# Linear attention ahead of a routed feed-forward: two of three key groups subtracted on GpSimd behind a ScalarE copy, and the attention's order planned anew

## The chip, the cores and the metric

The kernel runs on one core of one Trainium2 chip. The metric is the device time of one execution in microseconds (us). The engines are TensorE (PE), VectorE (DVE), ScalarE (ACT), GpSimd (POOL) and SyncE (SP, which here only issues transfers).

## The reference

For q, k, v of 8 batches, 8 heads, 576 positions and 64 columns, and a 64x128 matrix `w_phi`:

```python
def phi(x):
    proj = einsum('bhsd,df->bhsf', x, w_phi)
    proj = proj - max(abs(proj), axis=-1, keepdims=True)
    return concatenate([exp(proj), exp(-proj)], axis=-1)   # 256 features
q_p, k_p = phi(q), phi(k)
kv = einsum('bhsf,bhsd->bhfd', k_p, v)
z = sum(k_p, axis=2)
x = (q_p @ kv) / (q_p @ z + 1e-6)
```

Each of the 4608 rows of x (512 columns) is then given to one of 8 experts with a fixed capacity by its gate logits, and passes that expert's two-layer ReLU network. The change touches the attention alone.

## The kernel before

The attention works through 16 units, each two batches by two heads (the loop `for u in range(NU): unit(u)`). A unit's 576 positions are nine tiles of 64, taken in three groups of three (`SG`, line 134). For a unit:

- SP loads K and Q in pieces of 72 KB that already stand half transposed (`raw`, line 108), and V (`loadv`). Each has two buffers.
- DVE finishes the transposes of K and Q (`kT`, `qT`, line 158).
- PE projects a group of K or Q with `w_phi` into a pair of PSUM banks (line 169). All PSUM of this stage is four such pairs, `NG=4`.
- DVE takes the absolute maximum along the features (`kgm`, `qgm`, line 173) and subtracts it (`kgt`, `qgt`, line 176); both read the 128x768 projection from PSUM, and the subtraction gives the pair free.
- For K, ACT takes Exp of plus and minus `kgt` (`kP`, line 188); POOL adds the nine tiles up in eight additions (`ks`, lines 194 and 195); PE multiplies `kP` with V (line 204).
- For Q, PE transposes `qgt` (line 248) and ACT takes both Exps out of PSUM (`qP`, line 252).
- ACT copies the K-V product out of PSUM (`kvT`, line 208), PE turns it into the layout of the last product and appends the gate weights (`bd`, line 220), ACT copies that (`kz`, line 223); PE reduces `ks` over partitions (`z`, line 235), and DVE adds it to `kz` (line 237).
- PE forms numerator, denominator and logits (line 265); DVE divides (lines 269 to 280, `xp`); SP stores x; POOL sums the logits (lines 290, 292).

Units overlap. The order on each engine is made by the class `Plan`: each step has an engine, a duration in ns, a due time in us, steps that it depends on, and buffers that it takes and frees. `Plan.order` simulates the engines with these numbers and always takes the step that can start first, preferring early due times; the steps are then recorded in that order, and each engine runs its own list strictly in sequence. The due times are the constants of `ATT` (line 856): `TI` is the pitch of units, the others say where in a unit a step is due. Between the steps of units 1 to 3 stand 40 small steps (`init`, line 298) that build constants for the routing (lines 351 to 415): POOL makes a ramp, DVE casts or scales it. Behind the last unit of each pair of batches stand twelve DVE steps that prepare the routing (`pr`) and a count on PE.

Of the kernel before, what the change touches and what calls it, by code (L numbers as in the profile page):

```python
# [89 lines left out]
def attention(ctx, tc, nc, q, k, v, w_phi, w_gate, xs, L, C, xp, cfg={}, after=None, later=None, count=None, init=iter(())):  # L90

    B,H,S,D=q.shape
    NB=B//2; NP=H//2; NU=NB*NP
# [44 lines left out]
    def unit(u):  # L138
        bp,hp=divmod(u,NP)
        t0=u*d['TI']  # L140
        def add(name,eng,dur,due,fn,deps=(),mode=None,slot=(),frees=(),lat=None,after=0.):
            P.add((name,u),eng,dur,t0+due,fn,[(x,u) for x in deps],
                  lat={'PE':170.,'DVE':95.,'ACT':100.,'POOL':30.,'SP':0.}[eng] if lat is None else lat,mode=mode,slot=slot,frees=frees,after=after)
        def slots(*l): return tuple((kd,n,(kd,u) if len(z)==0 else (kd,u)+tuple(z)) for kd,n,*z in l)
        first=u==0
        if not first:
            add('ldk','SP',5200.,-d['ldk'],lambda x: loadx('k',k,u),slot=slots(('ki',2)),lat=4500.)
            add('ldq','SP',5200.,-d['ldq'],lambda x: loadx('q',q,u),slot=slots(('qi',2)),lat=4500.)
            add('ldv','SP',1300.,-d['ldv'],lambda x: loadv(u),slot=slots(('vi',2)),lat=4500.)
        else:  # L150
            for nm in 'kqv': add('ld'+nm,'SP',0.,-d['ldk'],lambda x: None,slot=slots((nm+'i',2)))

        def blocks(nm,aft):

            for bi in range(2):
                def f(x,bi=bi):
                    if bi==0: T[nm+'T',u]=sb.tile([128,2,9,32,2],F32,name=nm+'T',bufs=2)
                    V.transpose(T[nm+'T',u][:,bi].rearrange('p s t l -> p l s t'),T[nm,u][:,bi])
                add((nm+'t',bi),'DVE',640.,d[nm+'t']+.7*bi,f,['ld'+nm],slot=slots((nm+'T',2)) if bi==0 else (),frees=((nm+'i',u),),after=aft[bi] if first else 0.)
        def project(nm,g,s0,s1,due,src):  # L160
# [13 lines left out]
            def sub(x):  # L174
                t=T[nm+'t',u,g]=sb.tile([128,2,n,128],F32,name=nm+'t',bufs=3)
                V.tensor_sub(t,vw(),T[nm+'m',u,g].to_broadcast([128,2,n,128]))  # L176
# [4 lines left out]
        blocks('k',(7500.,8500.))  # L181
        for g,(s0,s1) in enumerate(SG):
# [6 lines left out]
            add(('ke',g),'ACT',2*ac(256*n,False),due+2.6,ex,[('kgs',g)],slot=slots(('kP',2)) if g==0 else (),frees=(('kgt',u,g),))  # L189
            def ad(x,s0=s0,s1=s1,g=g):  # L190
                if g==0: T['ks',u]=sb.tile([128,2,256],F32,name='ks',bufs=2)
                ks=T['ks',u]; kP=T['kP',u]
                for s in range(s0,s1):
                    if s==1: G.tensor_add(ks,kP[:,0],kP[:,1])  # L194
                    elif s>1: G.tensor_add(ks,ks,kP[:,s])  # L195
            add(('ad',g),'POOL',1300.*(n-(g==0)),due+4.,ad,[('ke',g)]+([('ad',g-1)] if g else []),frees=(('kP',u),),slot=slots(('ks',2)) if g==0 else ())
# [45 lines left out]
        for g,(s0,s1) in enumerate(SG):
# [10 lines left out]
            add(('T',g),'PE',2*n*109.+20.,due+d['T'],tr,[('qgs',g)],'A',slots(('g',NG,'T',g)),(('qgt',u,g),))  # L253
            add(('ex',g),'ACT',2*ac(256*n),due+d['T']+.8,ex,[('T',g)],slot=slots(('qP',d['nqP'],g)),frees=(('g',u,'T',g),))
        lastu=u==NU-1
        for g,(j0,j1) in enumerate(JG):
# [656 lines left out]
```

## Time and profile before

| what | us |
|---|---|
| median of 3 runs (809.74 to 812.13) | 810.55 |
| the profiled execution | 809.45 |
| its span, first to last instruction | 807.7 |
| PE busy in the span | 756.6 (94%) |
| DVE busy | 573.1 (71%) |
| ACT busy | 327.3 (41%) |
| POOL busy | 263.8 (33%) |
| first numerator of the attention (unit 0) starts | 33.60 |
| last numerator (unit 15) starts | 303.64 |

The first 310 us of the span are the attention, the rest routing and feed-forward. Shares over the whole span mix these stages: DVE is 94% busy in the attention's middle. A busy PE is not PE at its peak, since matmuls are pipelined and their ends are modelled; the distance from one burst to the next tells more. A line like `L176` is line 176 of the kernel before.

### The profile page before, as it was taken

The numbers are of one execution on the slowest core, as the hardware profiler recorded it, in microseconds if no ns is written. First come the engines' busy times: TensorE is split into PE (matmuls) and PEld (weight loads), VectorE is DVE, ScalarE is ACT, GpSimd is POOL, SyncE is SP. The second block draws the span as 40 slices with busy tenths as digits, with TensorE's granted clock in tenths as the row PEclk, the third lists the DMA queues.
The fourth block names the chain that finished last, engine by engine and source line by source line (L and its number), as shares of the span: only waits on it lengthen the run. The fifth ranks groups of instructions, "written<-read, shape, count | busy, mean of one in ns | idle before, by whom it ended". The sixth has DMA issues, their size and how long they took to land.

```text
span 807.7 us, 25190 instructions
## 1 busy us (share of the span) xinstructions
PE 756.6 (94%) x10718; PEld 653.4 (81%) x10718; DVE 573.1 (71%) x1407; ACT 327.3 (41%) x579; POOL 263.8 (33%) x295
## 2 busy tenths in 40 slices
PE   5888999999999996799999999999999999999995
PEld 3777887888888785488798798798898898897983
DVE  5798899999999885787686686586586685550400
ACT  2544555665554463143343243234334333441410
POOL 2664676655666560200401302203103104302011
PEclk9999999999999997699999999999999999999998
DMA  8868668668777311433424314405314424701300
GB/s 130 146 119 161 119 121 155 128 118 165 126 152 143 77 33 32 134 135 116 128 83 144 127 58 161 161 16 180 138 54 137 138 89 131 271 1 45 119 27 32
DMA packets 225344, 91.89 MB, mean 114 GB/s; under 512 B 191905, under 2 KB 208321, under 8 KB 225233
## 3 DMA queue, kind: packets, MB, share of 16 engines
q1 hardware_dynamic: 214400, 70.74, 37.5%
q0 software_dynamic: 6096, 18.97, 7.0%
q8 instruction: 84, 1.38, 0.7%
q10 hardware_dynamic: 4736, 0.59, 0.5%
q14 instruction: 28, 0.22, 0.1%
HBM read 71.39 MB, written 18.87 MB: 112 GB/s over the span
## 4 chain that ended last, share of the span: by engine, by line
PE 58%; issue 14%; DVE 10%; POOL 5%; SPq 5%; DMA 4%; ACT 3%; POOLq 0%; DVEq 0%; ACTq 0%
PE h L788 19%; PE y L817 17%; PE g L265 5%; SPq L114 4%; PE g L204 3%; PE g L169 3%; POOL ks L195 3%; PE y L832 2%; PE g L248 2%; ACT qP L252 2%; DMA qi<-in_q_dram 2%; PE h L763 2%; POOL out_dram L846 1%; PE rps L541 1%; DMA ki<-in_k_dram 1%
## 5 line engine op out<-in xcount | busy, mean ns | idle before, releaser
L195 POOL TENSOR_TENSOR ks<-ks,kP 128x512 f32<-128x512 f32 x112 | 142.8, 1275 | 9.9 <-ACT kP L188 1.3
L788 PE MATMUL h<-xh,w1h 128*128 128x272 f32 (+3 forms) x512 | 144.5, 303 | 0.2 <-DVE xl L766 0.2
L788 PE MATMUL h<-xh,w1l 128*128 128x272 f32 (+3 forms) x512 | 143.0, 299 | 0.0
L846 POOL DMA_INDIRECT out_dram<-ysb,idx x40 | 40.4, 1010 | 206.2 <-ACT ysb L840 166.7
L799 ACT ACTIVATE fh<-h 128x272 fp32r<-128x272 f32 (+2 forms) x128 | 49.2, 384 | 134.8 <-PE h L788 123.6
L817 PE MATMUL y<-w2h,fl 128*128 128x512 f32 x256 | 102.2, 399 | 0.0
L817 PE MATMUL y<-w2l,fh 128*128 128x512 f32 x256 | 101.9, 398 | 0.0
L817 PE MATMUL y<-w2h,fh 128*128 128x512 f32 x256 | 101.5, 397 | 0.0
L788 PEld LDWEIGHTS h<-xh,w1h 128*128 128x128 f32 x512 | 96.5, 189 | 2.1 <-issue 1.2
L758 POOL DMA_INDIRECT xg<-xs,idx x40 | 39.5, 987 | 177.2 <-issue 141.3
L788 PEld LDWEIGHTS h<-xh,w1l 128*128 128x128 f32 x512 | 96.7, 189 | 0.0
L803 DVE SCALAR_TENSOR_TENSOR fl<-h,fh 128x272 fp32r<-128x272 f32 (+2 forms) x128 | 52.8, 420 | 55.8 <-ACT fh L799 42.4
L788 PE MATMUL h<-xl,w1h 128*128 128x272 f32 (+3 forms) x512 | 91.8, 298 | 0.0
L188 ACT ACTIVATE kP<-kgt 128x768 f32<-128x768 f32 x96 | 74.5, 835 | 32.9 <-DVE kgt L176 32.5
L265 PE MATMUL g<-kz,qP 128*64 128x73 f32 x2304 | 77.6, 227 | 3.9 <-issue 2.1
L265 PEld LDWEIGHTS g<-kz,qP 128*64 128x64 f32 x2304 | 74.9, 136 | 7.6 <-issue 4.2
L252 ACT ACTIVATE qP<-g 128x768 f32<-128x768 f32 x96 | 71.9, 820 | 11.2 <-PE g L248 11.1
L788 PEld LDWEIGHTS h<-xl,w1h 128*128 128x128 f32 x512 | 75.6, 189 | 0.0
L204 PE MATMUL g<-kP,vi 64*64 64x256 f32 x1152 | 69.7, 382 | 2.4 <-DVE xp L280 1.3
L840 ACT COPY ysb<-y 128x512 f32<-128x512 f32 (+1 forms) x40 | 21.8, 544 | 101.1 <-PE y L817 70.9
L204 PEld LDWEIGHTS g<-kP,vi 64*64 64x64 f32 x1152 | 48.1, 135 | 13.8 <-issue 2.1
L194 POOL TENSOR_TENSOR ks<-kP 128x512 f32<-128x512 f32 x16 | 20.5, 1280 | 109.2 <-ACT kP L188 109.2
(179 smaller groups left out, 1329.2 us busy)
## 6 DMA issues: line engine op xcount, KB each, us to landing
raww<-in_moe_w_dram SPq DMA_DIRECT2D x64, 512.0 KB, 6.2
vi<-in_v_dram SPq DMA_DIRECT2D x32, 288.0 KB, 4.6
xs<-xp SPq DMA_DIRECT2D x32, 288.0 KB, 3.8
ki<-in_k_dram SPq DMA_DIRECT2D x124, 72.0 KB, 3.2
qi<-in_q_dram SPq DMA_DIRECT2D x124, 72.0 KB, 3.3
xg<-xs,idx POOLq DMA_INDIRECT x40, 3.6
out_dram<-ysb,idx POOLq DMA_INDIRECT x40, 3.5
ki<-in_k_dram ACTq DMA_DIRECT2D x4, 72.0 KB, 5.3
```

The source lines that it names most:

```text
L114: eng.dma_start(t[64*a+32*db:64*a+32*db+32,bi],o)
L188: for i in range(2): A.activation(o[:,:,:,128*i:128*i+128],t,AF.Exp,scale=1.0-2*i)
L195: elif s>1: G.tensor_add(ks,ks,kP[:,s])
L204: PE.matmul(p[64*a:64*a+64,i,0:256],v_[r,a,s,:],kP[r,s,a,:],start=s==0,stop=s==8,skip_group_check=True)
L252: for fh in range(2): A.activation(t[:,fh].rearrange('p a s t -> p a (s t)'),p,AF.Exp,scale=1.0-2*fh)
L265: PE.matmul(p[64*ab:64*ab+64,a,73*(j-j0):73*(j-j0)+73],T['qP',u,j//3][:,fh,a,j%3,64*ab:64*ab+64],T['kz',u][:,ab,fh,a,:],start=fh==0,stop=f ...
L758: G.indirect_dma_start(out=T['xg',r][0:n,bb,:],out_offset=None,in_=xs,in_offset=bass.IndirectOffsetOnAxis(ap=T['idx',r][0:n,bb,:],axis=0))
L788: PE.matmul(p,ws[:,k,o:o+128],xx[:,k,o1:o2],start=n==0,stop=n==11)
L799: A.activation(hh[:,f,o1:o1+m1],p[:,0:m1],AF.Relu)
L803: V.scalar_tensor_tensor(hl[:,f,o1:o1+m1],p[:,0:m1],0.0,hh[:,f,o1:o1+m1],op0=OP.max,op1=OP.subtract)
L817: PE.matmul(p,hx[:,f,o:o+128],ws[:,f%2,:],start=n==0,stop=n==23)
L846: st=G.indirect_dma_start(out=ov,out_offset=bass.IndirectOffsetOnAxis(ap=iv,axis=0),in_=yv,in_offset=None)
```

## The change

For the first two K groups of every unit but the first, the subtraction is split. ACT copies the projection from PSUM into `kgt` behind the maximum, which gives the PSUM pair free, and POOL subtracts the maximum from `kgt` in place (new lines 185 and 188). The third K group and the Q groups keep the DVE subtraction. In the plan, the additions on POOL become eight steps of their own with a due time `ad`; several durations are set anew; the steps `boot` and `aboot` count the first loads, by keeping SP and ACT occupied to 10.1 and 10.3 us; and all due times in `ATT` are new. New line numbers are 14 to 15 higher than old ones around the K groups.

```diff
+    P.add(('boot',-1),'SP',10100.,-1e3,lambda x: None)
+    P.add(('aboot',-1),'ACT',10300.,-1e3,lambda x: None)
+    POOLS=set(tuple(x) for x in d['pools']); NT=dict(kg=d['nkt'],qg=d['nqt'])
...
-            add((nm,g),'PE',n*218.+50.,due,pe,[(src[0]+'t',0),(src[0]+'t',1)],'Q',slots(('g',NG,nm,g)),((src,u),))
+            add((nm,g),'PE',n*218.,due,pe,[(src[0]+'t',0),(src[0]+'t',1)],'Q',slots(('g',NG,nm,g)),((src,u),))
             add((nm+'m',g),'DVE',dv(256*n),due+.8,mx,[(nm,g)])
-            add((nm+'s',g),'DVE',dv(256*n),due+1.6,sub,[(nm+'m',g)],slot=slots((nm+'t',3,g)),frees=(('g',u,nm,g),))
+            if (nm,g) in POOLS and not first:
+                def cp(x):
+                    t=T[nm+'t',u,g]=sb.tile([128,2,n,128],F32,name=nm+'t',bufs=NT[nm])
+                    A.copy(t.rearrange('p a s f -> p a (s f)'),T[nm+'p',u,g][:,:,0:128*n])
+                def gs(x):
+                    t=T[nm+'t',u,g]
+                    G.tensor_sub(t,t,T[nm+'m',u,g].to_broadcast([128,2,n,128]))
+                add((nm+'c',g),'ACT',ac(256*n),due+1.6,cp,[(nm+'m',g)],slot=slots((nm+'t',NT[nm],g)),frees=(('g',u,nm,g),))
+                add((nm+'s',g),'POOL',1450.,due+2.4,gs,[(nm+'c',g)])
+            else: add((nm+'s',g),'DVE',dv(256*n),due+1.6,sub,[(nm+'m',g)],slot=slots((nm+'t',NT[nm],g)),frees=(('g',u,nm,g),))
...
-            add(('ad',g),'POOL',1300.*(n-(g==0)),due+4.,ad,[('ke',g)]+([('ad',g-1)] if g else []),frees=(('kP',u),),slot=slots(('ks',2)) if g==0 else ())
+                add(('ad',s_),'POOL',1290. if s_ else 1.,due+d['ad']+1.3*(s_-s0),ad,[('ke',g)]+([('ad',s_-1)] if s_ else []),frees=(('kP',u),),slot=slots(('ks',2)) if s_==1 else ())
...
-ATT = {'TI': 16.83, 'ldk': 65.46, 'ldq': 71.93, ...
+ATT = {'TI': 16.73, 'ldk': 66.72, 'ldq': 64.38, ...
```

What this makes of the order is shown at two places. The first is the middle of the attention. This is PE there before, one unit; `g` with a number is a PSUM pair, and two rows that read `qgt` (transposes) and one `bd` follow.

```order
L169 MATMUL g_1815<-w,kT 64x128 x12
L235 MATMUL g_1834<-one,ks 64x2 x16
L248 MATMUL g_1853<-ident,qgt 128x128 x6
L169 MATMUL g_1863<-w,kT 64x128 x12
L169 MATMUL g_1888<-w,kT 64x128 x12
L265 MATMUL g_1906<-kz,qP 64x73 x40
L265 MATMUL g_1958<-kz,qP 64x73 x32
L169 MATMUL g_2007<-w,qT 64x128 x12
L169 MATMUL g_2035<-w,qT 64x128 x12
L204 MATMUL g_2048<-kP,vi 64x256 x12
L169 MATMUL g_2065<-w,qT 64x128 x12
L204 MATMUL g_2048<-kP,vi 64x256 x24
```

And this is PE now, one unit from its `bd` on; two rows of `w,kT` stand ahead of it.

```order
L234 MATMUL g_2919<-bd,kvT 64x72 x16
L172 MATMUL g_2938<-w,kT 64x128 x12
L249 MATMUL g_2958<-one,ks 64x2 x16
L172 MATMUL g_2977<-w,qT 64x128 x12
L172 MATMUL g_2996<-w,qT 64x128 x12
L172 MATMUL g_3015<-w,qT 64x128 x12
L279 MATMUL g_3039<-kz,qP 64x73 x40
L279 MATMUL g_3093<-kz,qP 64x73 x32
L262 MATMUL g_3144<-ident,qgt 128x128 x6
L262 MATMUL g_3151<-ident,qgt 128x128 x6
L262 MATMUL g_3168<-ident,qgt 128x128 x6
L218 MATMUL g_3177<-kP,vi 64x256 x36
```

All Q projections now stand ahead of the numerator, the three groups of transposes together behind it, and the K-V product in one piece at the end. `bd`, `z` and the numerator belong to the unit before. ACT in the same stretch before, one unit:

```order
L208 COPY kvT<-g_3100 128x512
L252 ACTIVATE qP<-g_3163 128x768 x2
L223 COPY kz<-g_3190 128x2x4x72
L252 ACTIVATE qP<-g_3177 128x768 x2
L252 ACTIVATE qP<-g_3255 128x768 x2
L188 ACTIVATE kP<-kgt 128x2x3x128 x6
```

And ACT now:

```order
L222 COPY kvT<-g_2826 128x512
L185 COPY kgt<-g_2887 128x768
L237 COPY kz<-g_2919 128x2x4x72
L185 COPY kgt<-g_2902 128x768
L200 ACTIVATE kP<-kgt 128x2x3x128 x6
L266 ACTIVATE qP<-g_3144 128x768 x2
L266 ACTIVATE qP<-g_3151 128x768 x2
L266 ACTIVATE qP<-g_3168 128x768 x2
```

The two new copies stand on both sides of `kz`, and K's Exps ahead of Q's. The second place is the constants, between the additions of units 1 and 2 on POOL. Before (`ktf`, `k_f`, `kl_f` and `e_f` are ramps, `L` the logits):

```order
L194 TENSOR_TENSOR ks<-kP 128x512
L195 TENSOR_TENSOR ks<-ks,kP 128x512 x4
L365 IOTA ktf 128x128
L195 TENSOR_TENSOR ks<-ks,kP 128x512 x3
L365 IOTA ktf 128x128 x2
L290 TENSOR_TENSOR L<-xp 128x72
L365 IOTA ktf 128x128 x3
L351 IOTA k_f 128x288
L351 IOTA kl_f 128x128
L351 IOTA k_f 128x18
L351 IOTA e_f 128x8
L194 TENSOR_TENSOR ks<-kP 128x512
```

Now, from the sixth addition of unit 1 (two subtractions of unit 1 stand ahead of its additions):

```order
L209 TENSOR_TENSOR ks<-ks,kP 128x512
L379 IOTA ktf 128x128 x2
L209 TENSOR_TENSOR ks<-ks,kP 128x512
L379 IOTA ktf 128x128
L365 IOTA k_f 128x288
L304 TENSOR_TENSOR L<-xp 128x72
L365 IOTA kl_f 128x128
L188 TENSOR_TENSOR kgt<-kgt,kgm 128x768
L365 IOTA k_f 128x18
L365 IOTA e_f 128x8
L188 TENSOR_TENSOR kgt<-kgt,kgm 128x768
L208 TENSOR_TENSOR ks<-kP 128x512
```

The subtractions of unit 2 now stand among the last constants. On DVE before, the constants (`kt`, `k`, `kl`) are spread between the groups of Q of unit 1 and end at the first maximum of unit 2 (`kgm`):

```order
L173 TENSOR_REDUCE qgm<-g_633 128x6
L366 TENSOR_SCALAR kt_681<-ktf 128x128
L176 TENSOR_TENSOR qgt<-g_633,qgm 128x768
L366 TENSOR_SCALAR kt_704<-ktf 128x128
L158 STREAM_TRANSPOSE qT<-qi 128x2x288
L366 TENSOR_SCALAR kt_733<-ktf 128x128
L158 STREAM_TRANSPOSE qT<-qi 128x2x288
L366 TENSOR_SCALAR kt_770<-ktf 128x128
L237 COPY kz<-g_737 128x8
L353 CAST k_788<-k_f 128x288
L353 CAST kl<-kl_f 128x128
L173 TENSOR_REDUCE kgm<-g_756 128x6
```

On DVE now, from the last `xp` of unit 0:

```order
L294 TENSOR_TENSOR xp<-g_563,rd 128x2x288
L380 TENSOR_SCALAR kt_636<-ktf 128x128
L161 STREAM_TRANSPOSE kT<-ki 128x2x288 x2
L380 TENSOR_SCALAR kt_670<-ktf 128x128
L161 STREAM_TRANSPOSE qT<-qi 128x2x288
L380 TENSOR_SCALAR kt_691<-ktf 128x128
L161 STREAM_TRANSPOSE qT<-qi 128x2x288
L380 TENSOR_SCALAR kt_709<-ktf 128x128
L380 TENSOR_SCALAR kt_713<-ktf 128x128
L380 TENSOR_SCALAR kt_731<-ktf 128x128
L367 CAST k_738<-k_f 128x288
L176 TENSOR_REDUCE kgm<-g_717 128x6
```

All six `kt` and the cast of `k_f` now stand between the last division of unit 0 and the first maximum of unit 2, with nothing of Q among them. On SP, the loads of K for unit 1 now stand ahead of those of Q.

More of the change, by code (lines that the diff above doesn't have):

```diff
@@ L140, in unit, with add @@
         t0=u*d['TI']
-        def add(name,eng,dur,due,fn,deps=(),mode=None,slot=(),frees=(),lat=None,after=0.):
+        def add(name,eng,dur,due,fn,deps=(),mode=None,slot=(),frees=(),lat=None,after=0.,seq=None):
             P.add((name,u),eng,dur,t0+due,fn,[(x,u) for x in deps],
-                  lat={'PE':170.,'DVE':95.,'ACT':100.,'POOL':30.,'SP':0.}[eng] if lat is None else lat,mode=mode,slot=slot,frees=frees,after=after)
+                  lat={'PE':170.,'DVE':95.,'ACT':100.,'POOL':30.,'SP':0.,'X':0.}[eng] if lat is None else lat,mode=mode,slot=slot,frees=frees,after=after,seq=seq and (seq,u))
         def slots(*l): return tuple((kd,n,(kd,u) if len(z)==0 else (kd,u)+tuple(z)) for kd,n,*z in l)
@@ L150, in unit @@
         else:
-            for nm in 'kqv': add('ld'+nm,'SP',0.,-d['ldk'],lambda x: None,slot=slots((nm+'i',2)))
+            for nm in 'kqv': add('ld'+nm,'X',0.,-d['ldk'],lambda x: None,slot=slots((nm+'i',2)))
         def blocks(nm,aft):
@@ L158, in f @@
                     V.transpose(T[nm+'T',u][:,bi].rearrange('p s t l -> p l s t'),T[nm,u][:,bi])
-                add((nm+'t',bi),'DVE',640.,d[nm+'t']+.7*bi,f,['ld'+nm],slot=slots((nm+'T',2)) if bi==0 else (),frees=((nm+'i',u),),after=aft[bi] if first else 0.)
+                add((nm+'t',bi),'DVE',640.,d[nm+'t']+.7*bi,f,['ld'+nm],slot=slots((nm+'T',2)) if bi==0 else (),frees=((nm+'i',u),),after=aft[u][bi] if u<len(aft) else 0.,seq=(nm+'t',0) if bi else None)
         def project(nm,g,s0,s1,due,src):
@@ L188, in ex, with ad @@
                 for i in range(2): A.activation(o[:,:,:,128*i:128*i+128],t,AF.Exp,scale=1.0-2*i)
[L189 to L193, printed above, removed]
+            add(('ke',g),'ACT',2*ac(256*n,False),due+2.6,ex,[('kgs',g)],slot=slots(('kP',2)) if g==0 else (),frees=(('kgt',u,g),),seq=('ke',0) if g else None)
+            for s_ in range(s0,s1):
+                def ad(x,s=s_):
+                    kP=T['kP',u]
+                    if s==0: return
+                    if s==1: T['ks',u]=sb.tile([128,2,256],F32,name='ks',bufs=2)
+                    ks=T['ks',u]
                     if s==1: G.tensor_add(ks,kP[:,0],kP[:,1])
-                    elif s>1: G.tensor_add(ks,ks,kP[:,s])
-            add(('ad',g),'POOL',1300.*(n-(g==0)),due+4.,ad,[('ke',g)]+([('ad',g-1)] if g else []),frees=(('kP',u),),slot=slots(('ks',2)) if g==0 else ())
+                    else: G.tensor_add(ks,ks,kP[:,s])
+                add(('ad',s_),'POOL',1290. if s_ else 1.,due+d['ad']+1.3*(s_-s0),ad,[('ke',g)]+([('ad',s_-1)] if s_ else []),frees=(('kP',u),),slot=slots(('ks',2)) if s_==1 else ())
             def kv(x,s0=s0,s1=s1,g=g):
@@ L252, in ex @@
                 for fh in range(2): A.activation(t[:,fh].rearrange('p a s t -> p a (s t)'),p,AF.Exp,scale=1.0-2*fh)
-            add(('T',g),'PE',2*n*109.+20.,due+d['T'],tr,[('qgs',g)],'A',slots(('g',NG,'T',g)),(('qgt',u,g),))
+            add(('T',g),'PE',2*n*109.-30.,due+d['T'],tr,[('qgs',g)],'A',slots(('g',NG,'T',g)),(('qgt',u,g),))
             add(('ex',g),'ACT',2*ac(256*n),due+d['T']+.8,ex,[('T',g)],slot=slots(('qP',d['nqP'],g)),frees=(('g',u,'T',g),))
@@ L301, in part @@
             def part(x): count(bp,ps.tile([128,2,512],F32,name='g%d'%x['buf'][('g',u,'cnt')],bufs=1)[0:32,0,0:8])
-            P.add(('cnt',u),'PE',1800.,t0+d['num']+25+N*d.get('prs',.7)+3,part,[(('pr',N-1),u)],lat=500.,mode='Z',slot=(('g',NG,('g',u,'cnt')),),frees=(('g',u,'cnt'),))
+            P.add(('cnt',u),'PE',800.,t0+d['num']+25+N*d.get('prs',.7)+3,part,[(('pr',N-1),u)],lat=500.,mode='Z',slot=(('g',NG,('g',u,'cnt')),),frees=(('g',u,'cnt'),))
     for u in range(NU): unit(u)
```

16 lines of the change are left out of this document (8 added, 8 removed).

## The prediction

> **What bounds the kernel now.** I first read the page's first line: the profiled execution took 809.45 us, of which 807.7 us is the span and 1.75 us lies around it. My sum is made against this execution, which stands 1.1 us under the 810.55 us median of the runs; the result is moved to the median at the end.
>
> ```profile
> span 807.7 us, 25190 instructions
> ```
>
> Only the attention is changed, so I took the busy time by stretch. 76.8 us is where unit 2's numerator starts on PE and 289.5 us where unit 14's starts, twelve units later; columns are the stretch, its length, then busy us and instructions of PE, PEld, DVE, ACT and POOL, the granted clock and the DMA share.
>
> ```profile
> 76.80:289.50 212.70, 202.69 (x5335) 175.62 (x5331) 199.83 (x335) 121.31 (x168) 129.05 (x117) 1.00 0.67 126
> ```
>
> A unit takes 212.7 / 12 = 17.72 us. PE and DVE both look full (95% and 94%). The timeline of PE decides which of them is: one unit, with start, duration, tiles and count, and any idle time before it in brackets.
>
> ```profile
> 161.28 0.89 PE L169 MATMUL g<-w,kT 64*64 64x128 f32 x24
> ...
> 164.77 4.79 PE L265 MATMUL g<-kz,qP 128*64 128x73 f32 x144 [0.33 <-DVE kgt L176]
> 169.49 1.54 PE L169 MATMUL g<-w,qT 64*64 64x128 f32 x48
> 170.85 1.47 PE L204 MATMUL g<-kP,vi 64*64 64x256 f32 x24
> 172.15 0.83 PE L169 MATMUL g<-w,qT 64*64 64x128 f32 x24
> 172.80 2.77 PE L204 MATMUL g<-kP,vi 64*64 64x256 f32 x48
> 175.50 1.53 PE L248 MATMUL g<-ident,qgt 128*128 128x128 f32 x12
> 176.96 0.73 PE L220 MATMUL g<-bd,kvT 64*64 64x72 f32 x32
> 177.51 0.59 PE L235 MATMUL g<-one,ks 64*64 64x2 f32 x32
> 178.04 0.89 PE L169 MATMUL g<-w,kT 64*64 64x128 f32 x24
> ```
>
> From one K projection to the next (161.28 to 178.04) this quick unit took 16.76 us, with 0.33 us idle for DVE's `kgt`. So PE can do a unit in 16.43 us, 1.3 us under the mean; what it loses, it loses to others. Next the groups of DVE instructions in the same twelve units (count, busy us, mean ns, idle before).
>
> ```profile
> L176 DVE TENSOR_TENSOR kgt<-g,kgm 128x768 f32<-128x768 f32 x37 | 34.5, 952 | 1.7
> ...
> L158 DVE STREAM_TRANSPOSE kT<-ki 128x576 f32<-128x576 f32 x24 | 17.8, 757 | 0.0
> ...
> L473 DVE TENSOR_TENSOR cmp<-dg,k 128x288 bf16<-128x288 bf16 x3 | 2.3, 776 | 0.0
> ```
>
> DVE reads PSUM for two operations of 0.95 us a group, six groups a unit. Its 199.83 us in twelve units are 16.65 us a unit, and it sits between every projection and everything behind it. I read DVE as the bound, with PE waiting in small pieces. ScalarE and GpSimd have room (121.31 / 12 = 10.1 and 129.05 / 12 = 10.8 us a unit).
>
> **The change part by part: the subtractions.** Two of a unit's six subtractions leave DVE, in 15 of 16 units. In the twelve units that is 24 x 0.95 = 22.8 us of busy time; DVE is left with (199.83 - 22.8) / 12 = 14.75 us a unit, below PE's 16.43. What was the bound is gone, and PE is late next.
>
> ScalarE and GpSimd get the work.
>
> ```profile
> L252 ACT ACTIVATE qP<-g 128x768 f32<-128x768 f32 x72 | 54.0, 819 | 6.0 <-PE g L248 6.0
> L223 ACT COPY kz<-g 128x576 f32<-128x576 f32 x12 | 7.8, 653 | 0.2 <-PE g L220 0.2
> ```
>
> The copy of 768 columns out of PSUM is not in the trace. Its bounds are `kz`'s 0.65 us (a copy, 576 columns) and `qP`'s 0.82 us (768 columns from PSUM, through Exp); I take 0.80, near the row of the same size. Two copies make ScalarE's unit 11.7 us, covered. The copy is in order behind the maximum: while it waits, `kz` of the unit before and the second copy stand behind it.
>
> ```profile
> L195 POOL TENSOR_TENSOR ks<-ks,kP 128x512 f32<-128x512 f32 x84 | 107.1, 1275 | 7.7 <-ACT kP L188 1.3
> L194 POOL TENSOR_TENSOR ks<-kP 128x512 f32<-128x512 f32 x12 | 15.4, 1281 | 78.5 <-ACT kP L188 78.5
> L292 POOL TENSOR_TENSOR L<-L,xp 128x72 f32<-128x72 f32 x18 | 6.1, 336 | 0.7
> ```
>
> The subtraction on GpSimd is not in the trace either. By proportion to the 512-column add it costs 1275 x 768 / 512 = 1.91 us; through the 72-column add (336 ns) and the 512-column one, the slope is 939 / 440 = 2.13 ns a column, so 1275 + 256 x 2.13 = 1.82 us. The plan writes 1.45 us, and a broadcast operand may be cheaper, so the bounds are 1.45 and 1.91, and I take 1.82. GpSimd's unit becomes 10.8 + 2 x 1.82 = 14.4 us busy; with 0.09 us idle ahead of each of its instructions (7.7 / 84), 15.4 us. It still ends before PE's unit does.
>
> One rule speaks against this. The Trainium skill (GPSIMD Engine Reference, "Performance versus the Vector engine") holds that a two-input elementwise operation takes GpSimd about 2.6 cycles an element, nearly twice VectorE's time, and advises VectorE. By its 4497 ns for 2048 columns the subtraction would be an estimated 1.69 us. The trace's rows agree on the factor of two; it costs nothing here as long as GpSimd has the time.
>
> **The new order, unit by unit.** In the new order a unit of PE runs two K projections, `bd` of the unit before, the third K projection, `z` of the unit before, three Q projections, the numerator, three transposes and KV in one piece. With the bursts above from start to start (0.68 a projection, 0.55 `bd`, 0.53 `z`, 4.72 numerator, 0.73 a group of transposes, 3.9 KV) and steps of 0.1 where another engine answers, counted from the unit's first projection: the first maximum runs 0.9 to 1.85, its copy 1.95 to 2.75, and frees the PSUM pair that `z` needs at 2.6, a wait of 0.2 us. The second copy ends at 4.05, before the third Q projection wants its pair. GpSimd subtracts 2.85 to 4.7 and 4.7 to 6.5, Exp of the first group is ready by 6.3, the eight adds, 1.36 us from one to the next, run to 17.4, and `z`, which is the next unit's at 16.4 + 2.8, finds them done with 1.8 us in hand. DVE works without a pause from the first maximum to the second `xp`, ending near 12.5, just when KV wants that PSUM pair: no wait, or 0.1. Transposes of the next inputs fill DVE to 15.3, and it idles to the next maximum.
>
> So PE sets the pace: 16.43, plus 0.2 at `z`, plus 0.2 of margin, since even the quick unit lost 0.33: 16.85 us. Three of the twelve units also carry the 0.78 us comparison for the routing count, and its matmuls, between maximum and second `xp`; I give them 1.0 us each. The stretch becomes 12 x 16.85 + 3.0 = 205.2 us. The old stretch and the tail behind it come from three rows.
>
> ```profile
> 76.80 4.79 PE L265 MATMUL g<-kz,qP 128*64 128x73 f32 x144
> ...
> 289.55 4.80 PE L265 MATMUL g<-kz,qP 128*64 128x73 f32 x144
> ...
> 303.64 5.04 PE L265 MATMUL g<-kz,qP 128*64 128x73 f32 x144
> ```
>
> Old: 289.55 - 76.80 = 212.75 us; the gain is 7.5 us. Bounds: with DVE's tail and `z` free of waits and no stalls, 16.45 a unit, gain 12; with waits on PSUM pairs of 0.15 us at each of the four bursts that follow a copy, 17.45 a unit, gain 0.4. The last numerator follows the one before by 14.09 us now; new it is 4.8 + 2.2 + 3.9 + 0.9 (`kvT`) + 0.6 + 0.6 + 0.6 = 13.6 us: a gain of 0.5 us. Behind it everything moves as it is.
>
> **The first loads and units 0 to 2.** The loads of K for unit 1 move ahead of those of Q on SP's queue. This changes which transposes can come first, but DVE is then busy with unit 0, which covers it. What matters is the start of GpSimd's adds of unit 1 and what stands behind them. Columns as before, GpSimd's rows first, then DVE's.
>
> ```profile
> 34.45 1.28 POOL L194 TENSOR_TENSOR ks<-kP 128x512 f32<-128x512 f32 x1 [5.97 <-ACT kP L188]
> ...
> 50.49 1.03 POOL L351 IOTA k_f<- 128x288 f32 x1
> ```
>
> ```profile
> 8.86 1.44 DVE L158 STREAM_TRANSPOSE kT<-ki 128x576 f32<-128x576 f32 x2 [5.09 <-DMA ki<-in_k_dram]
> ...
> 41.55 1.28 DVE L366 TENSOR_SCALAR kt<-ktf 128x128 bf16<-128x128 f32 x1 [2.54 <-POOL ktf L365]
> ...
> 46.57 0.22 DVE L366 TENSOR_SCALAR kt<-ktf 128x128 bf16<-128x128 f32 x1
> ...
> 52.65 0.96 DVE L173 TENSOR_REDUCE kgm<-g 128x6 f32<-128x768 f32 x1
> ...
> 75.64 0.96 DVE L173 TENSOR_REDUCE kgm<-g 128x6 f32<-128x768 f32 x1 [1.49 <-PE g L169]
> ```
>
> Old, the adds start at 34.45 and the last constants are made from 50.49. New, the two subtractions stand ahead of them. K of unit 0 is transposed by 10.3; DVE then waits 1.1 for the first projection and has twelve maxima and subtractions (0.9 each from start to start) and six transposes (0.72) before unit 1's first maximum, 26.5 to 27.5. ScalarE comes to the copy a little later, behind unit 0's last Exp, `kvT` and `kz`, which hang on DVE's last subtraction of unit 0 at 23.5 (2.4 for the rest of KV and the transposes, 1.6, 0.6, 0.6 for `bd`, 0.65, and 0.5 of steps): 29.9, the copy until 30.7, the subtractions until 34.4. So the adds start when they did. Eight adds (10.9), six `ktf` of 128 columns (0.46 each by proportion to `k_f`'s 288, 2.8) and the 1.03 us `k_f` put its end at 49.1. The queues are in order: in the new order the cast of `k_f` stands on DVE ahead of unit 2's first maximum, which therefore cannot start before 49.6, although by the replay of PE's row its projection is done near 45. PE loses about 4 us there.
>
> Old, that maximum is at 52.65 and unit 3's first at 75.64, 23.0 us later with 1.5 of idle time. New, the stretch loses two subtractions (1.9) and that idle time, and gains a wait of about 0.9 for the small `k_f`, which GpSimd makes only behind the subtraction, and about 1.0 of waits like that of the first `kt`, which took 1.28 us beside an add (0.22 when GpSimd was idle): 21.5 us. Unit 3's first maximum comes at 71.1 and unit 2's numerator, which the new order puts 4.6 us behind it, at 75.7 instead of 76.80: a gain of 1.1 us. Bounds: a gain of 4 if the cast of `k_f` does not hold the maximum, a loss of 3 if every small constant waits.
>
> The Trainium skill (SBUF — State Buffer, "SBUF: two separate sides") says that GpSimd and a two-port VectorE operation hold a shared port pair exclusively, the loser waiting out the whole instruction. The two `kt` rows agree; the transposes' 757 ns among adds do not show it for them.
>
> **Sum.** 7.5 + 0.5 + 1.1 = 9.1 us: 800.4 for the profiled execution, 801.4 against the median.
>
> **The rivals.** *A better pace* (0.13): the early hold does not happen and a unit takes 16.5 us; 12 x 0.35 and 4 us more, 793. For it: one unit did 16.76 with a wait in it. *PSUM pairs become the bound* (0.15): each of `z` and the Q projections waits for a copy behind a maximum, 17.45 a unit; with the early part from its middle to its bad end 810.55 - 0.4 - 0.5 - 1.1 = 808.6 to 812.7, mostly no change. For it: my replay has 0.1 us or less in hand at three of them; against it, a wait paid at `z` delays the bursts behind it, which then find their pairs free. *The port lock* (0.05): constants and routing steps, some 14 bursts, each wait 1.06 us (1.28 - 0.22) more because GpSimd is now rarely idle; 14 x 1.06 = 15 us of DVE, of which 12 units' slack hides half: 809, no change. Against it, the transposes, as many as before with GpSimd busy 61% of the time (129.05 / 212.7), took 757 ns. The Trainium skill's rule on the shared port pair, above, would do this. *GpSimd sets the pace* (0.07): adds, L and hand-over are 11.6 us a unit, and from a subtraction of (17.72 - 11.6) / 2 = 3.06 us on the kernel is slower; an in-place operation with a stride-0 operand at twice my price, 3.64, gives 18.9 a unit, 12 x 1.2 = 14 us, 810.55 + 14 = 825. Against it: the add of 72 columns in rows of eight costs no more than 336 ns, so short or strided rows have no steep price here.
>
> **How the numbers follow.** My forecast has 0.60 and its own range is 796 to 806. A measurement of this kernel can tell 0.3% from no change: 808.1 to 813.0 counts as the same. Faster: 0.60 + 0.13 and a third of the PSUM rival, 0.78. Same: the rest of that rival and the lock, 0.15; slower 0.07. The range leaves out the better pace's far half and GpSimd's case: 794 to 809.
>
> **What would show it.** Right: DVE near 177 us busy in twelve units, PE units of 16.7 to 17.0 us, POOL `kgt` near 1.8 us, DVE idle ahead of unit 2's first maximum with GpSimd's constants as releaser. Wrong: PE idle at `z` or the Q projections on ACT `kgt`; `z` waiting for POOL `ks`; a subtraction over 2.5 us; units of over 17.4 us.

## The result, and the profile of the changed kernel

The changed kernel took 804.23 us (median of 7 runs, 802.50 to 808.33), the kernel before 810.50 us beside it (7 runs, 807.75 to 812.42): a ratio of 0.9927, 95% interval 0.9901 to 0.9953, so 6 us less. The profiled execution took 803.38 us; its span is 801.4 us, 6.3 us shorter than before. The numerators of units 2, 14 and 15 are the marks that the prediction used. These are PE's rows (start, duration, count); the windows asked for cut these bursts short, so only their starts are compared.

```profile
74.42 0.79 PE L279 MATMUL g<-kz,qP 128*64 128x73 f32 x18
...
284.21 0.28 PE L279 MATMUL g<-kz,qP 128*64 128x73 f32 x2
...
297.68 0.54 PE L279 MATMUL g<-kz,qP 128*64 128x73 f32 x10 [0.39 <-ACT kz L237]
```

Before, they stood at 76.80, 289.55 and 303.64. So 76.80 - 74.42 = 2.4 us are won up to unit 2, (289.55 - 76.80) - (284.21 - 74.42) = 2.96 us in the twelve units between, and 14.09 - 13.47 = 0.6 us at the last one, 5.96 us in all. Behind the attention nearly nothing changes. The busy time of the twelve units, columns as in the prediction:

```profile
74.40:284.20 209.80, 199.68 (x5335) 177.21 (x5331) 183.54 (x310) 137.40 (x193) 164.27 (x142) 1.00 0.70 132
```

VectorE has lost 16 us and is 87% busy, TensorE 95%: VectorE is no longer the full one. The new operations, in the groups of these units:

```profile
L188 POOL TENSOR_TENSOR kgt<-kgt,kgm 128x768 f32<-128x768 f32 x25 | 36.2, 1470 | 35.1 <-ACT kgt L185 35.1
...
L185 ACT COPY kgt<-g 128x768 f32<-128x768 f32 x24 | 19.3, 808 | 14.0 <-DVE kgm L176 14.0
```

GpSimd subtracts in 1.47 us, ScalarE copies in 0.81. GpSimd stood idle for 35.1 us ahead of its subtractions and ScalarE for 14.0 us ahead of its copies, so neither is full. What VectorE and TensorE wait for there (total, times, longest):

```profile
DVE qT L161 <- DMA qi<-in_q_dram: 10.0, 6, 2.7
DVE kgm L176 <- PE g L172: 9.4, 9, 3.7
...
PE g L249 <- ACT kgt L185: 4.5, 11, 1.0
...
PE g L279 <- issue: 1.9, 5, 0.6
```

VectorE now waits for loads of q, which it did not before, and TensorE stands at `z` (line 249) for the copy in eleven of twelve units.

### The profile page after: what moved, and what is told of

It reads as the page before. It is cut to its first block, busy times and chain, and to the rows that moved or that the text cites. A ratio compares the mean times of both kernels' runs of the same rounds, so it can differ in the third digit from the quotient of the medians.

```text
span 801.4 us, 25172 instructions
## 1 busy us (share of the span) xinstructions
PE 751.3 (94%) x10718; PEld 652.3 (81%) x10718; DVE 555.4 (69%) x1377; ACT 347.9 (43%) x609; POOL 307.7 (38%) x325
## 4 chain that ended last, share of the span: by engine, by line
PE 64%; issue 13%; DVE 8%; POOL 4%; DMA 3%; ACT 3%; SPq 3%; POOLq 0%; DVEq 0%; ACTq 0%
PE h L802 20%; PE y L831 17%; PE g L218 6%; PE g L279 6%; PE g L172 4%; PE y L846 2%; PE g L262 2%; SPq L114 2%; DVE kgm L176 2%; PE h L777 2%; DMA qi<-in_q_dram 2%; POOL out_dram L860 1%; PE rps L555 1%; ACT kgt L185 1%; POOL ks L209 1%
## 5 line engine op out<-in xcount | busy, mean ns | idle before, releaser
L266 ACT ACTIVATE qP<-g 128x768 f32<-128x768 f32 x96 | 69.5, 827 | 48.4 <-PE g L262 48.4
L200 ACT ACTIVATE kP<-kgt 128x768 f32<-128x768 f32 x96 | 72.4, 831 | 12.1 <-POOL kgt L188 6.1
L218 PE MATMUL g<-kP,vi 64*64 64x256 f32 x1152 | 66.5, 379 | 1.2 <-DVE xp L294 0.7
L188 POOL TENSOR_TENSOR kgt<-kgt,kgm 128x768 f32<-128x768 f32 x30 | 43.5, 1470 | 43.7 <-ACT kgt L185 43.7
L218 PEld LDWEIGHTS g<-kP,vi 64*64 64x64 f32 x1152 | 45.2, 133 | 17.9 <-issue 2.2
```

What stands on the lines that cost most here:

```text
L188: G.tensor_sub(t,t,T[nm+'m',u,g].to_broadcast([128,2,n,128]))
L200: for i in range(2): A.activation(o[:,:,:,128*i:128*i+128],t,AF.Exp,scale=1.0-2*i)
L218: PE.matmul(p[64*a:64*a+64,i,0:256],v_[r,a,s,:],kP[r,s,a,:],start=s==0,stop=s==8,skip_group_check=True)
L266: for fh in range(2): A.activation(t[:,fh].rearrange('p a s t -> p a (s t)'),p,AF.Exp,scale=1.0-2*fh)
```

## The experiments

Each kernel was timed beside the kernel before on the same chip; the ratio to that is what is compared, and the changed kernel's is 0.9927. "The stretch" is unit 2's numerator to unit 14's: 212.75 us before, 209.79 in the changed kernel.

### The change in two halves

First the new order without the split: the changed kernel with an empty list of groups.

```
-pools=(('kg',0),('kg',1))
+pools=()
```

> The new plan and due times, but all six subtractions of a unit stay on VectorE; PE's order is the same as in the changed kernel. Theory (VectorE was the bound, and the time was won by taking 1.9 us a unit off it): VectorE is back at 16.6 us a unit, and in the new order its row from the first maximum to the second division grows from 12.5 to 14.4 us, so K times V starts 1.8 us later in every unit; units of 18.3 to 19 us, 812 to 822 us. Rival (the new order and the counted loads won it, the split adds little): 802 to 806 us.

It took 817.22 us, ratio 1.0099 (1.0075 to 1.0124); TensorE's order was the changed kernel's, row by row. Then the split without the new order: the kernel before, with the copy and the subtraction added and all due times left.

```
+if nm=='kg' and g<2 and not first:
...
+    add((nm+'c',g),'ACT',ac(256*n),due+1.6,cp,[(nm+'m',g)],...,frees=(('g',u,nm,g),))
+    add((nm+'s',g),'POOL',1450.,due+2.4,gs,[(nm+'c',g)])
+else: add((nm+'s',g),'DVE',...)
```

> The kernel before with nothing but the split: first two K groups copied by ScalarE and subtracted by GpSimd, with the old due times, loads and durations. Theory: VectorE has 1.9 us a unit less, units fall from 17.7 to about 17.2 us in the old order, which switches PE between kinds of matmul more often: 802 to 807 us. Rival (the order is what counts): 808 to 814 us.

It took 814.33 us, ratio 1.0064 (1.0043 to 1.0086). So each half alone is slower than the kernel before, by 1.0% and 0.6%, and the two together are faster by 0.7%. Neither half was given due times of its own: the first runs with those of the changed kernel, the second with those of the kernel before. The stretch of the first, and below it that of the second:

```profile
76.06:296.38 220.32, 207.40 (x5336) 176.87 (x5332) 198.31 (x333) 119.86 (x167) 127.40 (x116) 1.00 0.66 125
```

```profile
76.22:288.14 211.92, 203.61 (x5332) 176.17 (x5331) 181.96 (x310) 137.93 (x193) 164.06 (x141) 1.00 0.69 129
```

In the first VectorE has its 198 us again and the units take 18.4 us: the split is what lets the new order run. In the second VectorE is relieved of 18 us, but the stretch is only 0.8 us shorter than before (211.92 against 212.75), so in the old order VectorE's load alone did not hold the units. The waits name a price of the split. From its list of waits:

```profile
PEld g L244 <- POOL ks L204: 6.4, 12, 1.4
...
PE g L244 <- POOL ks L204: 3.4, 8, 1.1
```

In the old order `z` stands where GpSimd, which now subtracts before it adds, has not finished; in the kernel before, TensorE's `z` waited for it once, 0.9 us. That wait isn't in the list of the changed kernel. Since the stretch is no longer than before, what makes this execution longer lies behind it, and the last unit shows more than half of that:

```profile
302.81 0.64 PE L244 MATMUL g<-one,ks 64*64 64x2 f32 x32 [0.94 <-POOL ks L204]
303.84 6.42 PE L274 MATMUL g<-kz,qP 128*64 128x73 f32 x144 [0.39 <-DVE kz L246]
```

The last numerator starts 15.70 us after the one before (14.09 in the kernel before), 0.2 us later than there, and takes 6.42 us instead of 5.04, at a granted clock of 0.74 from 303.8 to 310.3 us, where the kernel before had 1.00. That is 1.6 of the 2.8 us between the two profiled executions (812.28 and 809.45 us).

Is `z` the whole of it? One number of the second kernel was changed, which makes `z` due later.

```
-'bd': -4.2, 'z': 0.71
+'bd': -4.2, 'z': 2.59
```

> The split alone in the old order (814.3 us) with one number changed: z is due 1.88 us later, which puts it one place further back in TensorE's row in about half of the units. Theory: the split alone lost because z stood where GpSimd, which now subtracts before it adds, had not finished the sums (waits of 9.8 us): 808 to 812 us, the waits of z for the sums under 5 us. Rival: other places of the old order cost as much, so a later z alone does not help: 813 to 816 us.

It took 814.10 us, ratio 1.0035 (1.0014 to 1.0055). The time lies in the rival's band, but on this chip the kernel before took 811.15 us, against 809.19 beside the second kernel; the ratio is a little lower than the second kernel's and the intervals overlap, so the run does not decide. In its list of waits (of the longest of its twelve executions, 822.73 us) `z` waits half as much for the sums:

```profile
PEld g L244 <- POOL ks L204: 3.2, 6, 0.8
```

At the last unit nothing changed: `z` again waited 0.94 us there and the last numerator again took 6.42. The place of `z` explains a part at most; the rest wasn't taken apart.

### One group instead of two

```
-pools=(('kg',0),('kg',1))
+pools=(('kg',0),)
```

> The changed kernel with one key group of three handed to ScalarE and GpSimd instead of two; the second group's subtraction is on VectorE again. With none handed over the time was 817.2 us, with two 804.2. Theory (VectorE binds first, then TensorE): the first group takes most of the gain, since 15 subtractions of 0.95 us are 14.3 us and TensorE's pace of 17.5 us a unit is met after that: 803 to 807 us. Rival (each group is worth the same, VectorE still in the chain with one): 809 to 812 us.

It took 809.35 us, ratio 0.9976 (0.9961 to 0.9991), the stretch 213.6 us. From none over one to two groups the ratios are 1.0099, 0.9976, 0.9927: the first group is worth 10 us, the second 4. The time lies in the rival's band, although the gain falls off as in the theory. VectorE is 90% busy in this stretch (192.09 of 213.64 us); that it still helps to set the pace is a reading of this number.

### Where the copy stands

ScalarE's copy waits for the maximum, though both only read the projection. Here the copy hangs on the projection alone, and both give the pair free.

```
-[(nm+'m',g)],slot=slots((nm+'t',NT[nm],g)),frees=(('g',u,nm,g),))
+[(nm,g)],slot=slots((nm+'t',NT[nm],g)),frees=(('g',u,nm,g),))
-add((nm+'s',g),'POOL',1450.,due+2.4,gs,[(nm+'c',g)])
+add((nm+'s',g),'POOL',1450.,due+2.4,gs,[(nm+'c',g),(nm+'m',g)])
```

> The changed kernel, but ScalarE's copy waits for the projection alone and runs beside the maximum; the PSUM pair is free when both are done. PE's order is the same. Theory (z waits 0.46 us a unit for the pair that the copy behind the maximum holds): the copy ends about 0.9 us earlier, the wait is gone in 14 units, 797 to 801 us. Rival (the next wait, for a pair or for instructions, takes its place): 803 to 805 us.

It took 825.79 us, ratio 1.0202 (1.0178 to 1.0226): the theory failed. VectorE's and ScalarE's rows of one unit show why (in this kernel the copy is line 186).

```profile
181.07 0.96 DVE L176 TENSOR_REDUCE kgm<-g 128x6 f32<-128x768 f32 x1 [2.93 <-PE g L172]
...
182.12 1.50 ACT L186 COPY kgt<-g 128x768 f32<-128x768 f32 x2 [1.19 <-DVE kgm L176]
...
183.72 1.82 DVE L176 TENSOR_REDUCE kgm<-g 128x6 f32<-128x768 f32 x2 [1.69 <-ACT kgt L186]
```

The first copy still waits for the first maximum, 1.19 us, and the second maximum now waits 1.69 us for the second copy, which came first in the program. Nothing runs side by side: reads of one PSUM pair by two engines are put in a row by semaphores. The Trainium skill (PSUM — Partial Sum Buffer, "PSUM bank collisions raise a hardware error") says that the compiler's scheduler makes two engines' accesses to one bank and quadrant depend on each other, reads among themselves too; this trace agrees, with 22.7 us of VectorE's maxima waiting for copies in the stretch. So the copy behind the maximum costs VectorE nothing, and the other order costs it a wait before the maximum of the next group.

### The constants

That the constants hold VectorE's first maximum of unit 2, as the prediction has it, is tested by eight constant steps ahead of everything and the others from 60 us on.

```
-P.add(('init',i),'DVE',300.,d['init']+i*d['pitch'],...)
+at=.2*i-20. if i<8 else 60.+2.*(i-8)
+P.add(('init',i),'DVE',300.,at,...,after=1e3*max(at,0.))
```

> The changed kernel, but the first eight constant steps (the ktf and the two larger ramps) stand ahead of the first transposes, where VectorE and GpSimd wait for the first loads, and the others from 60 us on. PE's order is the same. Theory (the cast of k_f held unit 2's first maximum, and VectorE's constants held that unit's transposes): PE's 3.5 us at z and 2.0 us at the transposes of units 1 and 2 go, 797 to 801 us. Rival (the lost time is made up later in any case, or the first loads are held instead): 803 to 806 us.

It took 803.75 us, ratio 0.9922 (0.9895 to 0.9949): no gain over the changed kernel. The hold itself was real: unit 2's numerator starts at 67.89 us, 6.5 us earlier. Half of that went again before unit 4's numerator, 20.32 us after unit 3's (16.75 in the changed kernel), where `z` waited 2.0 us for the copy and the granted clock was 0.72 from 101 to 107 us. Up to the last numerator 297.68 - 294.91 = 2.8 us were left:

```profile
294.91 0.79 PE L279 MATMUL g<-kz,qP 128*64 128x73 f32 x18 [0.39 <-ACT kz L237]
```

That is gone in one later window: 340 to 350 us of this kernel, and the same of the changed one below it; the figure before the last two is the granted clock.

```profile
340.00:350.00 10.00, 9.62 (x70) 9.06 (x70) 6.10 (x20) 2.12 (x5) 0.00 (x0) 0.66 0.46 151
```

```profile
340.00:350.00 10.00, 8.40 (x83) 7.70 (x82) 8.36 (x27) 3.55 (x9) 0.00 (x0) 1.00 0.17 58
```

Whether the dip came by chance in this execution or follows from the earlier start isn't settled; the median over nine runs shows no gain either.

### TensorE's wait at z

`z` needs eight columns, and the pair that `bd` holds has them free. It then waits for no copy, and the order on all engines stays.

```
-p=T['zp',u]=pair(('g',u,'z'))(x)
+p=T['zp',u]=T['bdp',u][:,:,504:512]
```

> The changed kernel, but the sums z are written into eight free columns of the PSUM pair that bd already holds, so z takes no pair of its own and cannot wait for the pair that ScalarE's copy frees; the order on every engine stays as it was. Theory: the pace of a unit was mis-sized (17.48 us against 16.85) because TensorE stands at z for the copy's pair, 4.5 us in the twelve steady units and 3.5 us more in the first; taking the wait away gives 4 to 7 us: 797 to 800 us, the stretch of twelve units near 205. Rival: the four pairs themselves are short, and the wait only moves to the next step that takes one (q projection or numerator): 802 to 805 us, the stretch still 208 to 211, with a new wait of TensorE for ScalarE or VectorE in z's place.

It took 807.27 us, ratio 0.9940 (0.9919 to 0.9962): no faster than the changed kernel. The profiled stretch is 206.5 us, 3.3 shorter, so the wait does cost pace, but a part moves to the next step that takes a pair, the Q projection:

```profile
PEld g L172 <- DVE kz L251: 4.8, 11, 0.5
```

The 3.3 us were lost again at both ends of that stretch: unit 2's numerator started at 78.04, 3.6 us late, with 0.50 as granted clock from 65 to 70 us, and the last one came 14.06 us after the one before, which leaves it 0.9 us later than in the changed kernel. The other 3.1 us between the two profiled executions (807.42 and 803.38) lie behind the attention, where the granted clock was 0.70 from 300 to 345 us and 0.96 from 345 to 390, against 0.73 and 1.00.

### The loads

> The changed kernel with the loads of k and q of every unit from the third on left out (the tiles of the first two units are used again, so part of the input is not read). Theory: the pace is partly set by the loads (VectorE's q transposes wait 10.0 us for them in the steady stretch, and some pauses of TensorE that the trace puts down to issue fall beside them): 796 to 800 us, the stretch of twelve units 203 to 206, the pauses shorter. Rival: VectorE has slack where it waits for a load and TensorE does not feel it: 802 to 805 us, the stretch 208 to 211.

```
 def loadx(nm,x,u):
+    if u>1: T[nm,u]=T[nm,u-2]; return
```

It took 799.36 us, ratio 0.9858 (0.9835 to 0.9881). The stretch is 4.9 us shorter than the changed kernel's; DMA falls from a share of 0.70 to 0.29.

```profile
74.20:279.09 204.89, 197.21 (x5336) 176.42 (x5332) 183.08 (x310) 137.39 (x193) 164.31 (x142) 1.00 0.29 70
```

Of the twelve units, the first takes 18.5 us in the changed kernel and 18.2 without the loads, the three with TensorE's routing count 17.9 and 17.8 in the mean, the other eight 17.2 and 16.7. The unit with the greatest difference on PE, in the changed kernel and below it without the loads:

```profile
144.91 1.10 PE L279 MATMUL g<-kz,qP 128*64 128x73 f32 x27
146.61 3.90 PE L279 MATMUL g<-kz,qP 128*64 128x73 f32 x117 [0.59 <-issue]
...
159.60 0.64 PE L249 MATMUL g<-one,ks 64*64 64x2 f32 x32 [0.46 <-ACT kgt L185]
160.06 1.32 PE L172 MATMUL g<-w,qT 64*64 64x128 f32 x37
161.75 1.31 PE L172 MATMUL g<-w,qT 64*64 64x128 f32 x35 [0.37 <-issue]
162.99 4.94 PE L279 MATMUL g<-kz,qP 128*64 128x73 f32 x144
```

```profile
143.47 5.00 PE L280 MATMUL g<-kz,qP 128*64 128x73 f32 x144
...
157.41 0.64 PE L250 MATMUL g<-one,ks 64*64 64x2 f32 x32 [0.32 <-ACT kgt L186]
157.87 2.26 PE L173 MATMUL g<-w,qT 64*64 64x128 f32 x72
160.06 1.16 PE L280 MATMUL g<-kz,qP 128*64 128x73 f32 x29
```

From numerator to numerator 162.99 - 144.91 = 18.08 us against 160.06 - 143.47 = 16.59. Two thirds of the 1.49 us are two pauses in which TensorE waited for nothing that the profile shows ("issue", 0.59 + 0.37), 0.14 is at `z`. So with the loads gone the pace is close to the one that was forecast, 16.85 us and 17.85 with routing.

How do loads cost TensorE time? The chain that ended last runs, in this unit, from SP's issues through the landing of q and VectorE's transpose to the maximum, the copy and `z`:

```profile
153.13 0.62 SPq L114
153.80 3.02 DMA qi<-in_q_dram
156.95 0.47 DVE qT L161
157.65 0.93 DVE kgm L176
158.66 0.81 ACT kgt L185
159.60 0.64 PE g L249 x32
```

And SP's row has hardly a pause:

```profile
165.48 5.92 SPq L114 DMA_DIRECT2D qi<-in_q_dram  x8
...
172.91 6.12 SPq L114 DMA_DIRECT2D ki<-in_k_dram  x8
179.12 6.43 SPq L114 DMA_DIRECT2D qi<-in_q_dram  x8
```

Twenty issues a unit, one behind the other: from the q of one unit (165.48) to the next (179.12) it took 13.6 us here, and the longest pause of this row from 76 to 263 us is 0.4. A k issue takes 0.63 us in the median but up to 3.7, so part of this time may itself be waiting. Three kernels took issues off SP, onto ScalarE:

```
-nc.sync.dma_start(t[64*i:64*i+64]...,o)                       # v
+(nc.sync if u==0 else nc.scalar).dma_start(t[64*i:64*i+64]...,o)
```

> The changed kernel with the two loads of v of each unit issued by ScalarE instead of SP; the order of the other engines stays. In the changed kernel SP issues without a pause from 76 to 263 us: sixteen issues of k and q, two of v and two stores of xs, 176 us of issuing and the rest of the stretch in the 0.1 us between them, 17.4 us a unit. Theory (SP's row of issues is the pace): two issues of 0.79 us less make 1.6 us a unit, the waits of VectorE for q go, and the time comes near that without the loads: 798 to 801 us, the stretch of twelve units 204 to 207. Rival (the transfers themselves are late, DMA 70% busy, or ScalarE's 1.6 us more a unit costs as much): 803 to 806 us, the stretch 208 to 212.

```
-for bi in range(2): raw(nc.sync,t,x,u,bi)
+for bi in range(2): raw(nc.scalar if bi and nm=='q' else nc.sync,t,x,u,bi)
```

> The changed kernel with the four issues of the second half of q of each unit on ScalarE instead of SP. Theory (SP's row is the pace): SP has 3 us less a unit and VectorE no longer waits for q: 797 to 801 us if ScalarE can take 3 us more (11.4 us busy of 17.5 in a unit becomes 14.4). Rival: ScalarE's copies and exponentials come later behind the issues, TensorE waits for ScalarE at z and at the sums kv: 803 to 809 us, with waits of TensorE for ScalarE over 10 us in the stretch.

The third was the first of them with the constants of the run above.

> The changed kernel with the loads of v issued by ScalarE and the constants built as in the run with the constants early (eight steps first, the others from 60 us). That run was 2.8 us ahead at the last numerator, but no faster at the end: TensorE's granted clock fell to 0.64 between 340 and 350 us, where the changed kernel had 1.00. Theory: with SP's row relieved both gains add, and the lost clock was one execution's chance: 795 to 799 us. Rival: the head start is lost again behind the attention part, whichever way it is won: 800 to 804 us.

They took 843.91, 860.04 and 849.75 us, ratios 1.0412, 1.0603 and 1.0477: far outside every expectation. ScalarE's rows of the first show it:

```profile
169.71 0.80 ACT L185 COPY kgt<-g 128x768 f32<-128x768 f32 x1
182.62 2.11 ACTq L120 DMA_DIRECT2D vi<-in_v_dram  x2
184.77 4.51 ACT L200 ACTIVATE kP<-kgt 128x768 f32<-128x768 f32 x6 [14.26 <-DMA qi<-in_q_dram]
```

ScalarE stood from 170.5 to 182.6 before it could issue v. In the trace the issues of SP and ScalarE use the same eight completion semaphores, taken in turn, and an issue waits until the transfer that used its semaphore before has landed. Here that was one that SP issued at 179.99 us, long after ScalarE had begun to stand, and it landed at 182.52. Alone on SP the transfer waited for is one eight places ahead. The other two kernels show the same, with 24.5 and 20.0 us in which ScalarE waited for loads of k and q. So these three tell nothing of SP's row. GpSimd's loads use other semaphores:

```
+(nc.gpsimd if u and i else nc.sync).dma_start(t[64*i:64*i+64]...,o)
```

> The changed kernel with one of the two loads of v of each unit issued by GpSimd instead of SP; TensorE, VectorE and ScalarE keep their orders. ScalarE as issuer stood still, because its issue waited for transfers that SP had not yet issued (6 to 14 us at a time). GpSimd's own load of the weights took 1.02 us to issue, and it has some 2 us to spare between its last sum and z. Theory (SP's row of issues sets the pace of 17.4 us a unit): SP has 0.79 + 0.1 us less a unit, so 16.6, and the stretch of twelve units comes to 203 to 207 instead of 209.8: 798 to 802 us. Rival: it is the transfers, not the issuing, that come late, or GpSimd's extra 1.0 us ends the sums after z is reached: 803 to 808 us, the stretch 208 to 213.

It took 807.54 us, ratio 0.9949 (0.9930 to 0.9969): the rival's time. The stretch:

```profile
74.69:283.37 208.68, 198.76 (x5336) 176.18 (x5332) 183.37 (x310) 137.74 (x193) 171.38 (x154) 1.00 0.69 131
```

And what is left of its waits:

```profile
PE g L279 <- issue: 3.6, 7, 1.0
PE g L249 <- ACT kgt L185: 3.5, 11, 0.3
```

VectorE no longer waits for q at all (10.0 us before), and `z` waits 3.5 us as without the loads. But the stretch is only 1.1 us shorter, because TensorE's pauses within the numerators grew from 1.9 to 3.6 us. So SP's row explains the waits for q; those waits are not what the loads cost. Counted from start to start of the same matmuls, the 4.9 us that the loads cost stand in the Q projections (3.1), at `z` (1.5) and in the numerators (0.4); this kernel wins back 2.0 and 1.4 us at the first two and loses 2.5 in the numerators.

TensorE's pauses without a releaser have an order of their own. In the changed kernel, without the loads and in this kernel they stand behind the same matmuls, the 1360th, 2249th, 4025th and 5802nd of the trace among them, and from one pause to the next it is always a multiple of 127 matmuls, to within two. The program's instructions are themselves transfers, and the changed kernel's stretch of 5335 matmuls has this row among its DMA queues (packets, MB, share):

```profile
q8 instruction: 42, 0.69, 1.3%
```

That is one packet for 127 matmuls. So the pauses fall where a new packet of instructions would begin, and they are longest while other transfers run: at most 0.3 us without the loads, 0.6 in the changed kernel, 1.0 in this one. That the loads delay the instructions is a reading of these counts, and no run tests it; nor do the pauses cover the whole 4.9 us. TensorE's idle time fell from 10.1 to 7.7 us without the loads, and the other half of the difference stands in its busy time, 199.68 against 197.21. That loads cost the stretch 4.9 us is shown; how they do it stays open. No run here beats the changed kernel beyond its interval, apart from the one that leaves loads out.

## Why the prediction was right, point by point

- **VectorE was the bound, and two subtractions less give the unit to TensorE.** Shown for the new order: with the subtractions back on VectorE and everything else kept the time is 817 us. Not shown for the kernel before: in its order the same relief shortened the stretch by 0.8 us only.
- **VectorE near 177 us busy.** 183.5. The subtractions took away 23 us as forecast; small routing steps gave 6 back (last section).
- **The prices.** The copy was put at 0.80 us and took 0.81. The subtraction was put at 1.82, between 1.45 and 1.91, and took 1.47, near the plan's figure; the broadcast operand came cheaper than proportion to the adds. It changes nothing, as GpSimd has room. The estimate from the Trainium skill (GPSIMD Engine Reference, "Performance versus the Vector engine"), 1.69 us, is 15% high against this row.
- **The pace: this is the term that was mis-sized.** 16.85 us a unit and 3.0 us for routing made 205.2 us for the stretch; it took 209.8, so the gain was 2.96 us, not 7.5. The step that failed is "PE sets the pace: 16.43, plus 0.2 at `z`, plus 0.2 of margin": 16.43 was read off one quick unit of the kernel before, and the margin of 0.2 had to stand for all that the loads do to TensorE. In the stretch the eight plain units took 17.2 us in the mean, where the forecast had 16.85. Without the loads the stretch is 204.9 us, the forecast to 0.3. The replay of VectorE, in which "transposes of the next inputs fill DVE to 15.3", also had every input on time, and VectorE waited 10.0 us for q; but the kernel without these waits won only 1.1 us in the stretch. The other side of the same term, 0.2 us at `z`, was 4.5 / 12 = 0.4 us, and 3.4 / 12 = 0.3 without the loads.
- **Pairs as the bound** (the rival at 17.45 a unit, 212.4 us for the stretch with 3.0 for routing). The stretch of 209.8 us lies between the forecast's 205.2 and that. The mechanism is there in part: with `z` in a place without a pair the profiled stretch was 3.3 us shorter, although the time was not; leaving out loads shortened both.
- **The last numerator** was forecast 13.6 us behind the one before, and came at 13.47.
- **The early part** was forecast to gain 1.1 us and gained 2.4. The mechanism is in the rows:

```profile
33.30 1.28 POOL L208 TENSOR_TENSOR ks<-kP 128x512 f32<-128x512 f32 x1 [0.26 <-ACT kP L200]
...
46.65 1.04 POOL L365 IOTA k_f<- 128x288 f32 x1
```

```profile
47.72 0.44 DVE L367 CAST k<-k_f 128x288 bf16<-128x288 f32 x1
48.08 1.81 DVE L176 TENSOR_REDUCE kgm<-g 128x6 f32<-128x768 f32 x2
```

```profile
50.06 1.03 PE L249 MATMUL g<-one,ks 64*64 64x2 f32 x32 [3.50 <-ACT kgt L185]
```

The cast of `k_f` does hold unit 2's first maximum, until 48.08 (forecast 49.6), the adds start at 33.30 (34.4), and TensorE loses 3.5 us at `z` (about 4). The first two came 1.5 and 1.1 us earlier, and that is the difference: from unit 2's first maximum to unit 3's, at 69.63, it then took the forecast 21.5 us.
- **The sum**, 9.1 us off the profiled execution, was 6.1. The time stayed well inside the range partly by luck: an early part that was better by 1.3 hid nearly a third of the 4.5 that the pace lacked.

## What to carry to other kernels

When the fullest engine is relieved, replay the next one with its inputs too: the transfers, whose cost was not seen as a term of its own while another engine was slow, belong into the sum with the same care as the engines. A pace read off one quick unit is close to the best case, not to the mean. Splitting work and re-ordering it each lost alone and won together here, so a trial of one of them says little about the pair. Before an issue is moved to another engine's row, look at which completion semaphores it shares, and with whom.

## What the hardware showed that was not expected

**Small VectorE steps beside GpSimd.** VectorE's rows of one routing count, in the changed kernel, and GpSimd's of the same time:

```profile
118.16 1.24 DVE L472 TENSOR_TENSOR di<-s,s 128x9 int32<-128x9 int32 x1
...
119.54 1.25 DVE L476 TENSOR_SCALAR dg<-di 128x9 bf16<-128x9 int32 x1
```

```profile
116.64 4.11 POOL L209 TENSOR_TENSOR ks<-ks,kP 128x512 f32<-128x512 f32 x3
```

Both steps, nine columns wide, took 0.16 us in the kernel before (0.156 and 0.160 in the median). Here they take 1.24 us beside GpSimd's additions, each ending about when an addition does. In the three counts of the stretch the two lines alone cost 6 x 1.09 = 6.5 us of VectorE. The kernel before had such steps on other lines: the comparison took 0.78 us there and 0.31 here, so the prediction's price for it probably held such a wait already. This is what the lock rival described, at less than half its 15 us; that it fell where VectorE had slack (87% busy) is a reading. The Trainium skill's rule on the shared port pair (SBUF — State Buffer, "SBUF: two separate sides") fits these rows, and the maxima and subtractions out of PSUM, 0.95 us beside additions as without, don't show it.

**The granted clock falls in places that differ from kernel to kernel.** In the changed kernel it was 0.50 between 50 and 55 us, behind the 3.5 us wait at `z`; in the kernel with the constants early, without that wait, it was 1.00 to 95 us, 0.72 between 101 and 107, behind a wait of 2.0 us at `z`, and 0.66 between 340 and 350. Not every wait is followed by such a fall: with half of v issued by GpSimd TensorE worked for 2.4 and 2.8 us only of 45 to 50 and of 50 to 55 us, and the clock stayed at 1.00 to 65 us. A few microseconds that one execution wins in the attention can so be lost behind it, and only medians over several runs tell.
